# Spectral filter and MLP on one core: filter products that read the transform's sums in PSUM, and the product's high part cast by ScalarE instead of VectorE

## Chip, cores, metric

One NeuronCore of a Trainium2 chip. The metric is the device time of one launch in microseconds, a median over runs; lower is better. The kernel before takes 2332.32 us (median of 3 runs, 2330.84 to 2332.87).

## What is computed

```python
x: (8, 3008, 256), filt_r, filt_i: (1505, 256), w_in: (256, 2048), w_out: (2048, 256)
X = np.fft.rfft(x, axis=1)
Y = X * (filt_r + 1j * filt_i)[None]
a = np.fft.irfft(Y, n=3008, axis=1).reshape(24064, 256)
h = a @ w_in
g = h / (1 + exp(-1.702 * h))
out = g @ w_out
```

All in fp32. A sequence of 3008 is transformed along 64 x 47 points: a first stage over 64, a second over 47, the product with the filter, and the two inverse stages.

## The kernel before

**MLP.** The 24064 tokens are 48 tiles (8 batches b, 6 tiles t each), of 512 columns, or 384 for t = 5 in batches 0, 2, 4 and 6. A tile has 16 chunks of the hidden width, fc. For each chunk TensorE (PE) makes six products into a PSUM tile `h` (L844), ScalarE (ACT) applies the activation twice, once rounded into `gh` (L848) and once in place in PSUM (L849), VectorE (DVE) subtracts the two into the low part `gl` (L850), and PE makes six products from `gh` and `gl` into two sums `o` (L869). Every operand of precision is split like this: a high part that TensorE reads as it is (type fp32r), and a low part that holds the rest.

**Transform of the next batch.** While PE works through the tiles of batch b - 1, a generator `fft(b)` is stepped between the chunks (a table of costs, `COSTS`, says after which chunk the next step is issued), so the transform of batch b runs beside the MLP. Its first stage (`packed`, for b > 1, or `thrice`) leaves `a_d` in DRAM. Its second stage has 16 groups i for each of 7 batches (112 in all), and `forward(i)` and `backward(i - 1)` alternate:

- `forward(i)`: two products `s2` on PE (k = 0, 1; L588 to L591), each with 48 useful rows on one side of the PSUM tile and the correction on the other. `merge` (L599, L600) has ACT copy the correction into `c_buf` and DVE add the sum into `c_buf`, in SBUF. DVE then multiplies with the filter in `f_buf`: L608 and L613 into `u_buf` (the parts with filt_i), L614 for both k at once into `c_buf` (filt_r). GpSimd (POOL) adds the two (L615). DVE casts the high part into `zy` (L619, once for each k), and POOL subtracts it for the low part (L620).
- `load(i + 2)` (L577, POOL's queue) brings the next input from `a_d`, and `load_f(i + 2)` the filter (SP's queue, L210).
- `backward(i)`: two products `i2` on PE, merged in the same way into `b`, which is stored to `b_d` from ACT's queue (L636).

**From a transform to its first tile.** When the last group of batch b is stored, `signal(b, 0)` or `turned_signal(b, 0)` makes the first tile of that batch: `br` is loaded from `b_d` (SP), split by ACT (L785) and POOL (L786), multiplied on PE into `i1` (L307 to L309), turned by DVE into `zt` (L794), sent through DRAM (`z_d`, then four loads of `y`, all on SP), and split by ACT (L726) and POOL (L727) into `y`. The first chunk of tile (b, 0), `h_b_0_0`, needs it.

**PSUM.** The tiles `s1`, `s2`, `i1` and `i2` share a ring of three banks (`ps_f`); `h` has three banks (two, and a shared one) from tile 6 on; the two `o` have one each.

**Order.** Instructions are issued by the Python code, and a scheduler at build time then sets the order in which they stand in each engine's queue; `keep_in_program_order` pins some of them. On the chip each queue is in order: an instruction that waits holds what stands behind it.

The change touches `forward` only.

Of the kernel before, what the change touches and what calls it, by code (L numbers as in the profile page):

```python
# [14 lines left out]
ALU = mybir.AluOpType  # L15
# [6 lines left out]
Q = 112  # L22
# [147 lines left out]
def tile_kernel(  # L170
# [9 lines left out]
    nc = tc.nc  # L180
# [17 lines left out]
    def ring(kind, shape, name):  # L198

        own = {"f": (ps_f, 3), "h": (ps_h, 2)}[kind]  # L200
        turn_of[kind] += 1
        if shared[0] == kind and turn_of[kind] % (own[1] + 1) == 0:
            return ps_x.tile(shape, F32, tag="x", name=name)
        return own[0].tile(shape, F32, tag=kind, name=name)
# [99 lines left out]
    zy = []  # L304
# [157 lines left out]
    def fft(b):  # L462
# [111 lines left out]
        def load(i):  # L574
            for k in range(2):
                src = a_d[k, 4 * i : 4 * i + 4].rearrange("q n d -> n q d")
                nc.gpsimd.dma_start(zy[0][64 * k : 64 * k + 48, i % 2].rearrange("p k s d -> p (k s) d"), src)  # L577

        def load_f(i):
            for k in range(2):  # L580
                load_in(f_buf[64 * k : 64 * k + 48, 2 * (i % 2) : 2 * (i % 2) + 2], fs[i])

        def second(i, m, src, name, k):

            pin = tc.keep_in_program_order
            ps = ring("f", [P, 2, D], f"{name}_{b}_{i}_{k}")
            if i == 0:
                pin(nc.tensor.matmul(ps[:, 0], de_sb[:, k, m + 1], src[:, k, 0], start=True, stop=True))  # L588
                nc.tensor.matmul(ps[:, 1], de_sb[:, k, m], src[:, k, 1], start=True, stop=True)
            else:  # L590
                pin(nc.tensor.matmul(ps, de_sb[:, k, m], src[:, k], start=True, stop=True))  # L591
            return ps

        def sides(k):
            return slice(64 * k, 64 * k + 48), slice(64 - 64 * k, 112 - 64 * k)

        def merge(k, ps, dst):
            h, o = sides(k)
            nc.scalar.copy(dst[h], ps[o])  # L599
            nc.vector.tensor_tensor(dst[h], ps[h], dst[h], ALU.add)  # L600

        def forward(i):

            u1, u2 = c_buf[i % 3], u_buf[i % 2]
            fr = f_buf[:Q, 2 * (i % 2) : 2 * (i % 2) + 2]
            f_r, f_i = fr[:, :, 0, :], fr[:, :, 1, :]
            merge(0, second(i, 0, zy[0][:, i % 2], "s2", 0), u1)
            nc.vector.tensor_tensor(u2[64:Q], u1[0:48], f_i[0:48], ALU.mult)  # L608
            yield
            merge(1, second(i, 0, zy[0][:, i % 2], "s2", 1), u1)  # L610
            if i + 2 < 16:
                load(i + 2)
            nc.vector.scalar_tensor_tensor(u2[0:48], u1[64:Q], -1.0, f_i[64:Q], ALU.mult, ALU.mult)  # L613
            nc.vector.tensor_tensor(u1, u1[:Q], f_r, ALU.mult)  # L614
            nc.gpsimd.tensor_tensor(u1, u1, u2, ALU.add)  # L615
            y = zy[0][:, 2 + i % 2]
            for k in range(2):
                h, o = sides(k)
                nc.vector.tensor_copy(y[h, k], u1[h])  # L619
                nc.gpsimd.tensor_tensor(y[o, k], u1[h], y[h, k].bitcast(F32), ALU.subtract)  # L620
            if i + 2 < 16:
                load_f(i + 2)
            yield
# [24 lines left out]
        for i in range(17):  # L648
            if i < 16:
                yield from forward(i)  # L650
            if i:
                yield from backward(i - 1)
# [367 lines left out]
```

## Time and profile before

| what | value |
|---|---|
| median of 3 runs | 2332.32 us (2330.84 to 2332.87) |
| profiled execution: its time | 2332.26 us |
| profiled execution: span of the instructions | 2330.2 us |
| DVE busy | 1622.9 us (70%), 2426 instructions |
| ACT busy | 1458.4 us (63%), 2686 instructions |
| POOL busy | 1155.2 us (50%), 1019 instructions |
| DMA | 293.44 MB, mean 126 GB/s |

The span runs from the first to the last instruction; 2.06 us of the execution's time lie outside it. Busy shares are means over the whole span; the transform of a batch takes part of it, the second stage of batches 1 to 7 lying between 177 us and 2026 us. A row of the profile gives the line of the kernel, the engine, the operation, `out<-in` by tile names without numbers, and a shape as partitions x elements. PEld is the load of TensorE's weights. An engine name with a q (ACTq, SPq) marks what its queue issues, DMAs above all.

### The profile page before, as it was taken

To read this page: it belongs to the slowest core of one execution; us is meant where nothing else is said; L and a number is where in the kernel's file an instruction comes from. 1 tells how busy PE (TensorE), PEld (TensorE's weight loads), DVE (VectorE), ACT (ScalarE), POOL (GpSimd) and SP (SyncE) were. 2 spreads that over 40 slices of the span, in tenths; PEclk is the share of its full clock that TensorE was granted. 3 is DMA by queue.
4 is the path that set the end of the run, shared out by engine and by line. 5 is a ranking of instruction groups with operands and counts; after the bars stand their busy time and mean duration, and the time that the engine had idled before them with its cause. 6 is when DMAs were issued, how large, how long until landed. Compare 5 with 4: busy or idle time off the path is not lost.

```text
span 2330.2 us, 32285 instructions
## 1 busy us (share of the span) xinstructions
PE 2321.9 (100%) x10620; PEld 1942.6 (83%) x10620; DVE 1622.9 (70%) x2426; ACT 1458.4 (63%) x2686; POOL 1155.2 (50%) x1019
## 2 busy tenths in 40 slices
PE   9999999999999999999999999999999999999999
PEld 7888898888888889888888888988888888888887
DVE  7978876688666885678856887568876688633332
ACT  6666667666675666756676666766657566555553
POOL 3035546466564665556654555636647365422220
PEclk9999999999999999999999999999999999999999
DMA  9265545556455654555545554555655465421200
GB/s 340 82 193 110 111 107 143 133 136 134 108 148 128 144 136 131 152 121 138 133 133 141 130 128 121 148 136 128 138 133 143 115 141 121 111 62 55 82 28 19
DMA packets 191958, 293.44 MB, mean 126 GB/s; under 512 B 18736, under 2 KB 127920, under 8 KB 191792
## 3 DMA queue, kind: packets, MB, share of 16 engines
q1 hardware_dynamic: 115088, 180.89, 27.1%
q0 software_dynamic: 46592, 44.05, 11.6%
q10 hardware_dynamic: 30112, 66.44, 11.1%
q8 instruction: 85, 1.39, 0.3%
q14 instruction: 81, 0.66, 0.1%
HBM read 176.49 MB, written 114.82 MB: 125 GB/s over the span
## 4 chain that ended last, share of the span: by engine, by line
PE 95%; DVE 2%; DMA 2%; ACT 1%; issue 1%; ACTq 0%; POOL 0%; SPq 0%; DVEq 0%; POOLq 0%
PE h L844 43%; PE o L869 43%; PE i L591 2%; PE s L591 2%; PE s L540 1%; PE i L309 1%; PE i L307 1%; PE i L308 1%; PE i L709 1%; DMA x<-in_x_dram 0%; DVE gl L850 0%; PE s L388 0%; DVE w_tu L277 0%; DMA fs<-f_y 0%; DMA w<-in_w_out_dram 0%
## 5 line engine op out<-in xcount | busy, mean ns | idle before, releaser
L844 PE MATMUL h<-y,wi 128*128 128x512 f32 (+1 forms) x4608 | 1178.2, 385 | 0.6 <-DVE gl L850 0.5
L844 PEld LDWEIGHTS h<-y,wi 128*128 128x128 f32 x4608 | 858.9, 188 | 166.0 <-DVE gl L850 1.9
L850 DVE TENSOR_TENSOR gl<-h,gh 128x512 fp32r<-128x512 f32 (+1 forms) x768 | 521.3, 679 | 487.4 <-ACT h L849 452.9
L869 PE MATMUL o<-gh,wo 128*128 128x512 f32 (+1 forms) x3072 | 838.7, 385 | 0.8 <-ACT gh L848 0.8
L848 ACT ACTIVATE gh<-h 128x512 fp32r<-128x512 f32 (+1 forms) x768 | 452.7, 589 | 583.7 <-PE h L844 448.5
L869 PEld LDWEIGHTS o<-gh,wo 128*128 128x128 f32 x3072 | 573.4, 188 | 111.2 <-ACT gh L848 1.5
L869 PE MATMUL o<-gl,wo 128*128 128x512 f32 (+1 forms) x1536 | 481.7, 385 | 0.5 <-DVE gl L850 0.5
L849 ACT ACTIVATE h<-h 128x512 f32<-128x512 f32 (+1 forms) x768 | 448.4, 584 | 0.0
L620 POOL TENSOR_TENSOR zy<-c_buf,zy 48x512 fp32r<-48x512 f32 x224 | 316.3, 1412 | 75.0 <-DVE zy L619 62.7
L869 PEld LDWEIGHTS o<-gl,wo 128*128 128x128 f32 x1536 | 287.5, 188 | 56.4 <-DVE gl L850 1.2
L615 POOL TENSOR_TENSOR c_buf<-c_buf,u_buf 112x512 f32<-112x512 f32 x112 | 144.8, 1293 | 229.8 <-DVE c_buf L614 229.8
L577 POOL DMA_DIRECT2D zy<-a_d x224 | 130.7, 588 | 232.0 <-PE s L591 92.5
L786 POOL TENSOR_TENSOR bl<-br,bh 128x512 fp32r<-128x512 f32 x70 | 94.5, 1363 | 201.5 <-ACT bh L785 168.5
L600 DVE TENSOR_TENSOR c_buf<-s,c_buf 48x512 f32<-48x512 f32 x224 | 154.1, 688 | 34.0 <-ACT c_buf L599 29.4
L599 ACT COPY c_buf<-s 48x512 f32<-48x512 f32 x224 | 130.4, 582 | 70.8 <-PE s L591 57.6
L599 ACT COPY b<-i 48x512 f32<-48x512 f32 x224 | 130.4, 582 | 58.2 <-PE i L591 46.4
L600 DVE TENSOR_TENSOR b<-i,b 48x512 f32<-48x512 f32 x224 | 153.8, 687 | 15.1 <-ACT b L599 10.2
L543 DVE TENSOR_TENSOR a<-s,a 64x512 f32<-64x512 f32 x144 | 99.0, 688 | 61.9 <-ACT a L542 58.7
L619 DVE CAST zy<-c_buf 48x512 fp32r<-48x512 f32 x224 | 109.7, 490 | 39.1 <-POOL c_buf L615 34.1
L727 POOL TENSOR_TENSOR y<-y 128x512 fp32r<-128x512 f32 (+1 forms) x76 | 92.6, 1225 | 59.5 <-ACT y L726 48.1
L608 DVE TENSOR_TENSOR u_buf<-c_buf,f_buf 48x512 f32<-48x512 f32 x112 | 109.2, 975 | 3.8
L542 ACT CAST a<-s 64x512 fp32r<-64x512 f32 x144 | 83.8, 582 | 40.7 <-PE s L540 28.6
(138 smaller groups left out, 1867.4 us busy)
## 6 DMA issues: line engine op xcount, KB each, us to landing
f_buf<-fs SPq DMA_DIRECT2D x224, 192.0 KB, 3.5
zy<-a_d POOLq DMA_DIRECT2D x224, 192.0 KB, 3.7
a_d<-a ACTq DMA_DIRECT2D x144, 256.0 KB, 3.0
x<-in_x_dram SPq DMA_DIRECT2D x47, 512.0 KB, 5.5
br<-b_d SPq DMA_DIRECT2D x94, 256.0 KB, 4.5
out_dram<-out SPq DMA_DIRECT2D x43, 512.0 KB, 3.5
b_d<-b ACTq DMA_DIRECT2D x112, 192.0 KB, 2.8
z_d<-zt SPq DMA_DIRECT2D x40, 512.0 KB, 2.7
```

What stands on the lines that cost most here:

```text
L577: nc.gpsimd.dma_start(zy[0][64 * k : 64 * k + 48, i % 2].rearrange("p k s d -> p (k s) d"), src)
L599: nc.scalar.copy(dst[h], ps[o])
L600: nc.vector.tensor_tensor(dst[h], ps[h], dst[h], ALU.add)
L608: nc.vector.tensor_tensor(u2[64:Q], u1[0:48], f_i[0:48], ALU.mult)
L615: nc.gpsimd.tensor_tensor(u1, u1, u2, ALU.add)
L619: nc.vector.tensor_copy(y[h, k], u1[h])
L620: nc.gpsimd.tensor_tensor(y[o, k], u1[h], y[h, k].bitcast(F32), ALU.subtract)
L844: ins = nc.tensor.matmul(ps[:, :w], wi_sb[half][:, wk, kc, c], y[:, yk, kc, :w], start=n == 0, stop=n == 5)
L848: nc.scalar.activation(gh[:, :w], ps[:, :w], AF.Gelu_apprx_sigmoid)
L849: gelu.append(nc.scalar.activation(ps[:, :w], ps[:, :w], AF.Gelu_apprx_sigmoid).ins)
L850: nc.vector.tensor_tensor(gl[:, :w], ps[:, :w], gh[:, :w].bitcast(F32), ALU.subtract)
L869: ins = nc.tensor.matmul(pos[m][:, :w], wb[:, P * m : P * m + P], g[:, :w], start=first_one, stop=last_one)
```

## The change

In `forward(i)` the sum is no longer moved to SBUF: DVE adds the correction in place, in the PSUM tile `ps` of the product. The three multiplications become four, of 48 rows each, which read the sum in PSUM and the filter in SBUF, and follow each k's sum at once. The two casts into `zy` go from DVE to ACT. The load of the next input is issued behind the multiplications of k = 1 rather than ahead of them.

```diff
             f_r, f_i = fr[:, :, 0, :], fr[:, :, 1, :]
-            merge(0, second(i, 0, zy[0][:, i % 2], "s2", 0), u1)
-            nc.vector.tensor_tensor(u2[64:Q], u1[0:48], f_i[0:48], ALU.mult)
-            yield
-            merge(1, second(i, 0, zy[0][:, i % 2], "s2", 1), u1)
+            for k in range(2):
+                h, o = sides(k)
+                ps = second(i, 0, zy[0][:, i % 2], "s2", k)
+                nc.scalar.copy(u1[h], ps[o])
+                nc.vector.tensor_tensor(ps[h], ps[h], u1[h], ALU.add)
+                if k:
+                    nc.vector.scalar_tensor_tensor(u2[o], ps[h], -1.0, f_i[h], ALU.mult, ALU.mult)
+                else:
+                    nc.vector.tensor_tensor(u2[o], ps[h], f_i[h], ALU.mult)
+                nc.vector.tensor_tensor(u1[h], ps[h], f_r[h], ALU.mult)
+                if k == 0:
+                    yield
             if i + 2 < 16:
                 load(i + 2)
-            nc.vector.scalar_tensor_tensor(u2[0:48], u1[64:Q], -1.0, f_i[64:Q], ALU.mult, ALU.mult)
-            nc.vector.tensor_tensor(u1, u1[:Q], f_r, ALU.mult)
             nc.gpsimd.tensor_tensor(u1, u1, u2, ALU.add)
             y = zy[0][:, 2 + i % 2]
             for k in range(2):
                 h, o = sides(k)
-                nc.vector.tensor_copy(y[h, k], u1[h])
+                nc.scalar.copy(y[h, k], u1[h])
                 nc.gpsimd.tensor_tensor(y[o, k], u1[h], y[h, k].bitcast(F32), ALU.subtract)
```

Since a scheduler sets the order, the queues change in more places than the diff shows. Lines behind the change move by six (L844 becomes L850, L848 becomes L854, L869 becomes L875).

ACT's queue in batch 4, from chunk 8 of tile (3, 2) on (`gh_3_2_8` is the high part of chunk 8; `s2_4_4_0` the product of group 4, k = 0). Before:

```order
L848 ACTIVATE gh_3_2_8_10004<-h_3_2_8_9997 128x512
L849 ACTIVATE h_3_2_8_9997<-h_3_2_8_9997 128x512
L599 COPY c_buf1_83<-s2_4_4_1_9960 48x512
L848 ACTIVATE gh_3_2_9_10028<-h_3_2_9_10021 128x512
L849 ACTIVATE h_3_2_9_10021<-h_3_2_9_10021 128x512
L599 COPY b_4_1_9906<-i2_4_3_0_9993 48x512
L599 COPY b_4_1_9906<-i2_4_3_1_10015 48x512
L636 DMA b_d4_9505<-b_4_1_9906 48x1024
L848 ACTIVATE gh_3_2_10_10066<-h_3_2_10_10059 128x512
```

And now:

```order
L610 COPY c_buf1_83<-s2_4_4_0_10007 48x512
L610 COPY c_buf1_83<-s2_4_4_1_10013 48x512
L854 ACTIVATE gh_3_2_9_10081<-h_3_2_9_10074 128x512
L855 ACTIVATE h_3_2_9_10074<-h_3_2_9_10074 128x512
L599 COPY b_4_1_9958<-i2_4_3_0_10046 48x512
L854 ACTIVATE gh_3_2_10_10120<-h_3_2_10_10113 128x512
L855 ACTIVATE h_3_2_10_10113<-h_3_2_10_10113 128x512
L642 DMA b_d4_9553<-b_4_1_9958 48x1024
L625 CAST zy_1451<-c_buf1_83 48x512 x2
L599 COPY b_4_1_9958<-i2_4_3_1_10068 48x512
L854 ACTIVATE gh_3_2_11_10138<-h_3_2_11_10131 128x512
```

The two casts of group 4 now stand between the activations of chunks 10 and 11, with a copy behind them.

PE's queue where tile (2, 5) ends and tile (3, 0), the first that needs the transform of batch 3, begins (`o_2_5` are the sums of the old tile, `s1_4` products of the first stage of batch 4). Before:

```order
L540 MATMUL s1_4_2_1_8829<-e1_4_2_8752,t1_two_3258 128x512
L844 MATMUL h_3_0_0_8842<-y_3_0_8479,wi_0_583 128x512
L869 MATMUL o_2_5_0_8495<-gl_2_5_13_8769,wo_1_984 128x384
L869 MATMUL o_2_5_1_8496<-gl_2_5_13_8769,wo_1_984 128x384
L869 MATMUL o_2_5_0_8495<-gh_2_5_14_8788,wo_1_984 128x384
```

And now:

```order
L540 MATMUL s1_4_2_0_8848<-e0_4_2_8773,t1_two_3274 128x512
L875 MATMUL o_2_5_0_8543<-gl_2_5_15_8867,wo_1_984 128x384
L875 MATMUL o_2_5_1_8544<-gl_2_5_15_8867,wo_1_984 128x384
L540 MATMUL s1_4_2_1_8877<-e1_4_2_8800,t1_two_3274 128x512
L850 MATMUL h_3_0_0_8890<-y_3_0_8527,wi_0_583 128x512
L850 MATMUL h_3_0_1_8916<-y_3_0_8527,wi_0_583 128x512
L850 MATMUL h_3_0_2_8955<-y_3_0_8527,wi_0_583 128x512
L540 MATMUL s1_4_3_0_8940<-e0_4_3_8853,t1_two_3274 128x512
```

The first product of tile (3, 0) stood ahead of the last 14 products into the old tile's sums; now it stands behind all of them. From the last inverse product of batch 3, `i2_3_15_1`, to that first product the queue holds 166 matmuls of 384 columns and 19 of 512 before, and 122 and 13 now.

SP's queue in the same stretch. Before:

```order
L210 DMA br_3_0_8480<-b_d3_6817 64x4x256 x2
L210 DMA z_d_3_0_8620<-zt_3_0_8567 128x1024
L210 DMA y_3_0_8479<-z_d_3_0_8620 32x8x128
L210 DMA x_4_2_8677<-in_x_dram 128x1024
L210 DMA y_3_0_8479<-z_d_3_0_8620 32x8x128 x3
```

And now:

```order
L210 DMA br_3_0_8528<-b_d3_6849 64x4x256 x2
L210 DMA z_d_3_0_8668<-zt_3_0_8615 128x1024
L210 DMA x_4_2_8725<-in_x_dram 128x1024
L210 DMA y_3_0_8527<-z_d_3_0_8668 32x8x128 x4
L210 DMA br_3_1_8806<-b_d3_6849 64x4x256 x2
```

The load of `x_4_2` moves from behind the first of the four loads of `y` to ahead of all four.

## Rows read from the trace of the kernel before

**Rows 1.** The page, part 1: TensorE's busy time, share and instructions.

```profile
PE 2321.9 (100%) x10620; PEld 1942.6 (83%) x10620; DVE 1622.9 (70%) x2426; ACT 1458.4 (63%) x2686; POOL 1155.2 (50%) x1019
```

**Rows 2.** Busy time by stretch: us, PE, PEld, DVE, ACT, POOL, granted clock, DMA.

```profile
177.00:333.00 156.00, 155.30 (x741) 131.79 (x741) 131.77 (x207) 97.42 (x180) 84.23 (x79) 1.00 0.50 111
722.00:888.00 166.00, 166.00 (x740) 137.91 (x739) 142.76 (x206) 105.05 (x193) 101.39 (x94) 1.00 0.56 130
177.00:2026.00 1849.00, 1848.30 (x8360) 1549.55 (x8360) 1377.85 (x2039) 1193.72 (x2180) 1052.45 (x932) 1.00 0.54 130
```

**Rows 3.** Timeline, 1041 to 1049 us: start, duration, engine, line, operation, [idle before].

```profile
1041.06 1.52 PE L844 MATMUL h<-y,wi 128*128 128x512 f32 x6
1041.93 0.68 DVE L600 TENSOR_TENSOR c_buf<-s,c_buf 48x512 f32<-48x512 f32 x1 [0.31 <-ACT c_buf L599]
1042.42 0.62 PE L869 MATMUL o<-gl,wo 128*128 128x512 f32 x2
1042.62 0.60 ACT L848 ACTIVATE gh<-h 128x512 fp32r<-128x512 f32 x1 [0.72 <-DVE c_buf L600]
...
1047.41 0.39 PE L591 MATMUL i<-zy,de_sb 128*128 128x512 f32 x1
...
1048.99 0.84 PE L869 MATMUL o<-gh,wo 128*128 128x512 f32 x3
```

**Rows 4.** Groups by line and shape: count, busy us, mean ns, idle before and its releaser.

```profile
L600 DVE TENSOR_TENSOR c_buf<-s,c_buf 48x512 f32<-48x512 f32 x224 | 154.1, 688 | 34.0 <-ACT c_buf L599 29.4
L619 DVE CAST zy<-c_buf 48x512 fp32r<-48x512 f32 x224 | 109.7, 490 | 39.1 <-POOL c_buf L615 34.1
L608 DVE TENSOR_TENSOR u_buf<-c_buf,f_buf 48x512 f32<-48x512 f32 x112 | 109.2, 975 | 3.8
L613 DVE SCALAR_TENSOR_TENSOR u_buf<-c_buf,f_buf 48x512 f32<-48x512 f32 x112 | 88.8, 793 | 3.4
L614 DVE TENSOR_TENSOR c_buf<-c_buf,f_buf 112x512 f32<-112x512 f32 x112 | 85.2, 760 | 1.9
L528 ACT CAST e<-x 64x512 fp32r<-64x512 f32 x72 | 44.6, 620 | 11.8 <-POOL e L529 8.9 <-POOL x L522 1.4
L457 DVE SCALAR_TENSOR_TENSOR u_buf<-s,f_y 48x512 f32<-48x512 f32 x8 | 5.5, 693 | 0.2
```

**Rows 5.** Timeline, 186.7 to 189.5 us, of POOL, DVE and PE.

```profile
186.79 3.02 POOL L620 TENSOR_TENSOR zy<-c_buf,zy 48x512 fp32r<-48x512 f32 x2
187.01 1.66 DVE L613 SCALAR_TENSOR_TENSOR u_buf<-c_buf,f_buf 48x512 f32<-48x512 f32 x1
188.71 0.69 DVE L850 TENSOR_TENSOR gl<-h,gh 128x512 fp32r<-128x512 f32 x1
189.45 1.66 PE L844 MATMUL h<-y,wi 128*128 128x512 f32 x6 [0.46 <-DVE gl L850]
```

**Rows 6.** Timeline, 887.9 to 921.2 us, the chain from batch 3's transform to tile (3, 0).

```profile
887.91 0.40 PE L591 MATMUL i<-zy,de_sb 128*128 128x512 f32 x1
...
890.17 0.31 ACTq L636 DMA_DIRECT2D b_d<-b  x1
897.38 1.14 ACT L785 CAST bh<-br 128x512 fp32r<-128x512 f32 x2 [1.40 <-DMA br<-b_d]
904.62 0.70 DVE L794 STREAM_TRANSPOSE zt<-i 128x512 f32<-128x512 f32 x1
905.35 0.34 SPq L210 DMA_DIRECT2D z_d<-zt  x1
909.35 1.90 SPq L210 DMA_DIRECT2D y<-z_d  x3
918.05 0.62 ACT L726 CAST y<-y 128x512 fp32r<-128x512 f32 x1
919.66 2.55 POOL L727 TENSOR_TENSOR y<-y 128x512 fp32r<-128x512 f32 x2
921.20 0.40 PE L844 MATMUL h<-y,wi 128*128 128x512 f32 x1
```

**Rows 7.** DMA issues, 903 to 922 us: KB each, median us from issue to landing.

```profile
y<-z_d SPq DMA_DIRECT2D x4, 128.0 KB, 5.0
```

**Rows 8.** The same of 1757 to 1774 us, where batch 6 hands over.

```profile
y<-z_d SPq DMA_DIRECT2D x4, 128.0 KB, 2.9
```

## The prediction

> **What bounds the kernel.** I read the page's engine shares first: TensorE is busy for 2321.9 us of the 2330.2 us span, the others 70% or less [rows 1]. A busy share of PE can mislead, so the timeline comes next. Six products of 512 columns start at 1041.06 and the seventh at 1042.42, 0.2267 us apiece with no gap [rows 3]. Then the stretches: from 177 us (where the second stage of the first transform that the change touches begins) to 2026 us, PE is without work for 1849.00 - 1848.30 = 0.70 us, at a granted clock of 1.00, which is the 2.4 GHz level [rows 2]. The changed lines issue the same products with the same columns. So the time is this row of products plus the gaps in it, and the change can give back 0.7 us at most; all that can move the time upwards is a product that comes to wait. By DVE's 142.76 us of 166.00 in a second stage against ACT's 105.05 [rows 2], DVE is the fuller of the two, yet neither sets the time.
>
> **The change, part by part.** I work against the profiled execution, 2332.26 us, which is 0.06 us under the median.
>
> *DVE, per group.* Before: two sums of 688 ns, 975 and 793 and 760 for the three multiplications, two casts of 490 [rows 4]: 4884 ns. After: two sums and four multiplications of 48 rows. The trace has the same multiplication from PSUM in the first transform, 693 ns [rows 4]. A sum that is written to PSUM has no row on DVE; I bound it by the 688 ns of the same sum into SBUF and by the 975 of the dearest operation here, and take 688, since shape and inputs are the same. 2 x 688 + 4 x 693 = 4148 ns, so DVE saves 0.74 us a group, 82 us over 112 groups. PE's products cover all of it: worth nothing by itself. At 975 the saving is 18 us, and the cover is the same.
>
> *ACT, per group.* Two casts of 620 ns, the row of a cast from SBUF to SBUF [rows 4], come on: 139 us over the kernel. In a second stage of 16 groups ACT goes from 105.05 to 105.05 + 16 x 1.24 = 125 of 166 us, and DVE from 142.76 to 131. Again no engine is full. The casts bring a wait: on DVE they waited 34.1 us in all for POOL's addition [rows 4]. Now ACT waits, with the copy of an inverse product and the activations behind it. What hides it: `gh` of a chunk ended at 1042.62 + 0.60 = 1043.22 and was first used two chunks later, at 1048.99, 5.8 us of margin [rows 3]. Two casts (1.24) and the mean wait per group (34.1 / 112 = 0.3) fit. Taken as nothing.
>
> *The sums' stay in PSUM.* `s2` of k = 0 was free when its sum ended, 1041.93 + 0.68 = 1042.61; the ring of three comes back to that bank with the fourth product, at 1047.41, 4.8 us later [rows 3]. Two multiplications more are 1.4 us; 3.4 are left. Taken as nothing, up to 1 us in some groups if a `gl` comes in between. The Trainium skill, "PSUM — Partial Sum Buffer", section "Summary: rules for kernel authors", speaks against the change: "Evacuate promptly — 2 MiB is tight". By that rule PE would be held by the ring and the sum would grow; the 4.8 us above are the row against it.
>
> *POOL and SP.* They issue what they issued. `load` stands behind two more multiplications in the code, but its wait is for the product on PE, as before.
>
> *A collision that goes.* L613, 793 ns on average [rows 4], took 1.66 us at 187.01 while POOL's subtraction ran; `gl` was late and PE waited 0.46 us at 189.45 [rows 5]. The new multiplications read one operand from PSUM, as the sums of L600 do, which keep to 688 ns beside the same POOL [rows 4]. I take -0.5 us.
>
> *The hand-over from a transform to its first tile.* This is where the change costs. The transform ends later in PE's queue, so less work stands between its last product and the first product that needs its result. For batch 3 the queue held 166 products of 384 and 19 of 512 columns there, which took 921.20 - 887.91 = 33.29 us [rows 6]; with 0.2267 for the wide ones, a narrow one is (33.29 - 4.31) / 166 = 0.1746 us. Now there are 122 and 13: 21.30 + 2.95 = 24.2 us of cover. The chain that has to fit, step by step [rows 6 to 8]: the product to `br` split, 887.91 to 897.38, 9.5 us (up to 0.9 more, as ACT's store of `b_d` now stands behind a chunk's activations); on to the end of `zt`, 904.62 + 0.70, 7.9; from `z_d`'s issue at 905.35 to the last issue of `y`, 909.35 + 2/3 x 1.90 = 910.6, 5.3, or 4.6 now that no load of `x` stands between the four; its landing, 5.0 beside other loads, 2.9 without; the first split of `y`, 0.62. From 25.6 to 29.3 us. I take 27.2 (half of the ACT delay, 4.6, a landing of 4.0, since the load of `x_4_2` now runs just ahead): 3.0 us more than the cover. Behind the first product, the second of chunk 0 comes after three others, 0.9 us, but needs POOL's half, 2.55 / 2 = 1.3: 0.4 more. **+3.4 us.** In the order before, products of the old tile filled that hole; now the old tile has none left.
>
> *The other hand-overs.* Counted alike, batches 4 and 6 have 138 products of 512 (31.3 us), batch 5 has 156 and 13 (30.2), batch 7 has 156 and 7 (28.8), against 25.6 to 29.3: mostly covered, +0.3 in all. Batches 1 and 2 don't go through `z_d`; nothing.
>
> **Sum:** 2332.26 - 0.5 + 3.4 + 0.3 = 2335.5, and with the bounds of the hand-over (1.3 to 5.1 short) 2333.4 to 2337.6. All the guesses of that chain lean towards waiting, so I forecast 2335.0. A difference under 0.2% (4.7 us) can't be told from no change, so this is "within".
>
> **The rivals.**
>
> 1. *The hand-over of batch 3 holds longer: slower.* SP's queue is in order, and the load of `x_4_2` now stands ahead of all four loads of `y`. If its buffer is not free when `z_d` has landed, or if it takes the transfers' time from them, each microsecond goes straight into PE's hole. It decides once batch 3 loses 5.2 us or more (4.7 + 0.5): the long end of the chain (5.1 + 0.4) already does, 2337.5, and 3 us of SP waiting gives 2340.5. For it: the landing of 5.0 us beside such a load [rows 7] against 2.9 [rows 8]. Against it: the load has the time of `z_d`'s own landing to get out of the way. Chance 0.22.
> 2. *The hand-over fits after all.* If `y` lands in 2.9 us and POOL gets to its part at once, the shortfall is near 1 us and the freed collision pays for half: 2331.7 to 2332.4. `y` was split at 918.05, in ACT's order, perhaps well after it lands [rows 6]. Chance 0.10.
> 3. *ACT holds the activations.* A cast that waits for POOL's addition delays two chunks' `gh`. It needs more than 5.8 us of delay in a row [rows 3]; if one group in ten lost 1 us, 2343. Chance 0.05.
> 4. *The ring holds PE.* With the 3.4 us of margin used up in one group of ten and 1 us lost in each, again 2343. Chance 0.03. (It is where the page quoted above would lead.)
> 5. *Faster by over 0.2%.* Rows 2 leave 0.7 us to gain; only an error of reading allows it. Chance 0.03.
>
> The forecast has the remaining 0.57; with rival 2, within 0.2%: 0.67. Slower: 0.22 + 0.05 + 0.03 = 0.30. Faster: 0.03. The range runs from 2331.3 (rival 2 and the spread of runs) to 2340 (most of rival 1); the forecast's own is 2332.5 to 2337.
>
> **What the profile after would show.** DVE near 1541 us busy, ACT near 1597; the multiplications at 684 to 700 ns without the long ones; L620 on POOL shorter than before, with fewer collisions. PE without a gap but near 925 us, where it waits some 3 us for ACT's or POOL's split of `y`, and nothing of the like at the other batches. Wrong would be: PE waiting for an activation in the middle of a second stage (rivals 3, 4), SP's load of `x` waiting ahead of `y` (rival 1), or no wait at 925 us at all (rival 2).

## The result, and the profile after

The changed kernel takes 2352.44 us (median of 4 runs, 2350.91 to 2353.04), the one before beside it 2332.6 (2330.84 to 2333.09): a ratio of 1.0085, with an interval of 1.0068 to 1.0103. It is **slower, by 20 us**. The forecast was 2335.0 and no difference that can be measured, with a range up to 2340.0; both were wrong.

The page of the kernel after, part 1, as in [rows 1]:

```profile
PE 2331.3 (99%) x10620; PEld 1942.7 (83%) x10620; DVE 1542.3 (66%) x2314; ACT 1593.2 (68%) x2910; POOL 1116.2 (47%) x1019
```

The loads of the engines came out as worked out (DVE 1541, ACT 1597), and the durations within 2%. These are the groups that answer to [rows 4]; the sum written to PSUM has a row now, 700 ns:

```profile
L611 DVE TENSOR_TENSOR s<-s,c_buf 48x512 f32<-48x512 f32 x224 | 156.9, 700 | 30.4 <-ACT c_buf L610 24.5
L616 DVE TENSOR_TENSOR c_buf<-s,f_buf 48x512 f32<-48x512 f32 x224 | 154.2, 688 | 3.0
L613 DVE SCALAR_TENSOR_TENSOR u_buf<-s,f_buf 48x512 f32<-48x512 f32 x112 | 77.6, 693 | 3.6
L625 ACT CAST zy<-c_buf 48x512 fp32r<-48x512 f32 x224 | 138.5, 619 | 85.6 <-POOL c_buf L621 81.9
```

VectorE has 81 us less to do, and the kernel is 20 us longer. Where they went is read by stretches, as in [rows 2] (us, PE, PEld, DVE, ACT, POOL, granted clock, DMA share, GB/s):

```profile
177.00:333.00 156.00, 153.69 (x729) 129.37 (x728) 125.74 (x189) 114.02 (x207) 77.22 (x76) 1.00 0.50 111
722.00:888.00 166.00, 166.00 (x739) 137.76 (x738) 120.98 (x179) 119.25 (x215) 88.92 (x89) 1.00 0.60 119
890.00:905.00 15.00, 14.01 (x74) 12.56 (x74) 10.95 (x18) 11.36 (x24) 5.95 (x5) 1.00 0.51 161
924.00:941.00 17.00, 12.42 (x41) 8.79 (x40) 11.24 (x17) 9.44 (x19) 12.84 (x11) 0.80 0.79 242
941.00:1180.00 239.00, 239.00 (x1060) 198.01 (x1059) 167.56 (x247) 170.88 (x305) 130.83 (x123) 1.00 0.57 125
1180.00:1240.00 60.00, 58.55 (x254) 46.94 (x253) 35.21 (x53) 42.36 (x77) 35.42 (x28) 1.00 0.52 148
1750.00:1812.00 62.00, 59.52 (x257) 47.39 (x256) 35.85 (x53) 42.66 (x78) 35.72 (x28) 1.00 0.51 144
```

Most of the second stage runs full (722 to 888, 941 to 1180). PE lacks work in the second stage of batch 1, at the end of the later ones, and above all where batches 3, 4 and 6 hand over to their first tile (924 to 941, 1180 to 1240, 1750 to 1812).

**A ledger for all that follows.** Between the starts of two successive products of PE lie 0.2267 us for 512 columns [rows 3], or 0.1733 for 384, when PE is full. All time beyond that, summed over the products, I call lost (the few products of other widths, nearly all of them in the start, count with their usual step; only the level of the start hangs on that). It is 18.6 us before and 38.9 after; the difference, 20.3, is that of the spans (2350.5 - 2330.2), so the ledger holds everything. It is taken from the one profiled execution of each kernel, while the column of medians is over all its runs. It is split by place: the start (to 177 us), batch 1's transform (177 to 400), the hand-overs (from the last inverse product of batch 2, 3, ... to 15 us behind the first product of its first tile), and the rest. Lost us:

| kernel | median us | start | batch 1 | hand-overs | rest |
|---|---|---|---|---|---|
| before | 2332.6 | 15.4 | 1.6 | 1.0 | 0.6 |
| after | 2352.4 | 15.7 | 3.6 | 15.5 | 4.1 |
| e1 casts on VectorE | 2353.0 | 15.6 | 5.1 | 17.3 | 2.6 |
| e2 casts alone | 2334.3 | 15.7 | 3.3 | 1.1 | 0.7 |
| e3 paced | 2339.9 | 15.4 | 4.0 | 3.1 | 3.5 |
| e4 four banks | 2347.3 | 15.5 | 3.7 | 1.0 | 13.2 |
| e5 before, four banks | 2338.2 | 15.3 | 1.6 | 1.2 | 6.4 |
| e6 sums in SBUF | 2351.0 | 16.4 | 7.3 | 2.4 | 13.5 |
| e7 split product | 2351.4 | 15.5 | 7.1 | 2.7 | 12.7 |
| e8 paced, casts on VectorE | 2335.9 | 15.5 | 4.7 | 1.9 | 1.5 |
| e9 before, paced | 2334.3 | 15.3 | 1.6 | 1.3 | 2.9 |
| e10 low half on VectorE | 2350.0 | 15.8 | 4.0 | 11.3 | 5.8 |
| e11 banks held | 2382.2 | 15.8 | 4.2 | 34.1 | 17.0 |
| e12 split by columns | 2337.4 | 15.3 | 4.2 | 2.4 | 0.6 |

Of the 20.3 us the hand-overs took 14.5 (batch 3 8.9, batch 4 2.4, batch 6 3.4, the others nothing), the rest of the second stages 3.5, batch 1 2.0, the start 0.3.

**Batch 3's hand-over**, 903 to 941 us, in the timeline, which answers to [rows 6]:

```profile
903.61 0.39 PE L591 MATMUL i<-zy,de_sb 128*128 128x512 f32 x1
912.79 1.14 ACT L791 CAST bh<-br 128x512 fp32r<-128x512 f32 x2 [2.61 <-DMA br<-b_d]
920.01 0.70 DVE L800 STREAM_TRANSPOSE zt<-i 128x512 f32<-128x512 f32 x1
920.75 0.34 SPq L210 DMA_DIRECT2D z_d<-zt  x1
921.13 0.43 SPq L210 DMA_DIRECT2D x<-in_x_dram  x1
923.71 2.76 SPq L210 DMA_DIRECT2D y<-z_d  x4
...
926.67 0.98 PE L875 MATMUL o<-gh,wo 128*128 128x384 f32 x4 [0.39 <-ACT gh L854]
...
928.52 0.47 PE L540 MATMUL s<-e,t_two 128*128 128x512 f32 x1 [0.24 <-DVE a L544]
929.68 1.27 POOL L529 TENSOR_TENSOR e<-x,e 64x512 fp32r<-64x512 f32 x1
930.03 1.14 ACT L732 CAST y<-y 128x512 fp32r<-128x512 f32 x2 [0.24 <-DMA y<-z_d]
930.64 0.47 PE L540 MATMUL s<-e,t_two 128*128 128x512 f32 x1 [1.00 <-DVE a L544]
930.95 0.86 PE L850 MATMUL h<-y,wi 128*128 128x512 f32 x3
931.02 1.28 POOL L522 TENSOR_TENSOR ev<-x 128x512 f32<-128x512 f32 x1
932.38 1.27 POOL L529 TENSOR_TENSOR e<-x,e 64x512 fp32r<-64x512 f32 x1
932.67 0.47 PE L540 MATMUL s<-e,t_two 128*128 128x512 f32 x1 [0.86 <-DVE a L544]
933.72 2.50 POOL L733 TENSOR_TENSOR y<-y 128x512 fp32r<-128x512 f32 x2
935.04 6.28 PE L850 MATMUL h<-y,wi 128*128 128x512 f32 x15 [1.90 <-DMA out_dram<-out]
941.16 1.07 PE L875 MATMUL o<-gh,wo 128*128 128x512 f32 x4
```

From the last inverse product to the first of tile (3, 0) the chain took 930.95 - 903.61 = 27.34 us; 33.29 us of queue stood there before [rows 6], now 24.1 us of products and 3.3 us lost. None of PE's waits in these 3.3 us is put down to `y`: they are for an activation of the old tile (0.39) and for VectorE's part in the next batch's first stage (0.24, 1.00). `y` would not have been there earlier, though: its first split starts at 930.03 and takes about 0.6 us, so the two waits end together, at about 930.6, and no run parts them. That hole had been seen, and a second had not. The low half of `y` is POOL's, and when the first split was done, POOL was in the first of three first-stage instructions of the next batch, and the two others stood ahead of `y`'s: 933.72 instead of soon after 930.6. PE's next products start at 935.04, and the wait that the profile puts down to a store is really for this half: the first of its two instructions ends about 933.72 + 2.50 / 2 = 934.97.

### The profile page after: what moved, and what is told of

Read it like the earlier page. It is cut to its first block, busy times and chain, and to the rows that moved or that the text cites. A ratio compares the mean times of both kernels' runs of the same rounds, so it can differ in the third digit from the quotient of the medians.

```text
span 2350.5 us, 32421 instructions
## 1 busy us (share of the span) xinstructions
PE 2331.3 (99%) x10620; PEld 1942.7 (83%) x10620; DVE 1542.3 (66%) x2314; ACT 1593.2 (68%) x2910; POOL 1116.2 (47%) x1019
## 3 DMA queue, kind: packets, MB, share of 16 engines
q1 hardware_dynamic: 115088, 180.89, 27.2%
q8 instruction: 85, 1.39, 0.3%
## 5 line engine op out<-in xcount | busy, mean ns | idle before, releaser
L850 PE MATMUL h<-y,wi 128*128 128x512 f32 (+1 forms) x4608 | 1184.0, 386 | 4.7 <-DVE gl L856 2.3
L850 PEld LDWEIGHTS h<-y,wi 128*128 128x128 f32 x4608 | 860.4, 188 | 174.7 <-DVE gl L856 6.3
L875 PE MATMUL o<-gh,wo 128*128 128x512 f32 (+1 forms) x3072 | 839.6, 385 | 4.0 <-ACT gh L854 4.0
L854 ACT ACTIVATE gh<-h 128x512 fp32r<-128x512 f32 (+1 forms) x768 | 452.6, 589 | 436.8 <-PE h L850 364.0
L875 PEld LDWEIGHTS o<-gh,wo 128*128 128x128 f32 x3072 | 573.0, 188 | 116.2 <-ACT gh L854 7.0
L875 PE MATMUL o<-gl,wo 128*128 128x512 f32 (+1 forms) x1536 | 483.1, 385 | 0.9 <-DVE gl L856 0.9
L875 PEld LDWEIGHTS o<-gl,wo 128*128 128x128 f32 x1536 | 287.2, 188 | 57.3 <-DVE gl L856 2.5
L626 POOL TENSOR_TENSOR zy<-c_buf,zy 48x512 fp32r<-48x512 f32 x224 | 288.3, 1287 | 91.1 <-ACT zy L625 78.5
L600 DVE TENSOR_TENSOR b<-i,b 48x512 f32<-48x512 f32 x224 | 153.4, 685 | 67.3 <-ACT b L599 63.0
L625 ACT CAST zy<-c_buf 48x512 fp32r<-48x512 f32 x224 | 138.5, 619 | 85.6 <-POOL c_buf L621 81.9
L792 POOL TENSOR_TENSOR bl<-br,bh 128x512 fp32r<-128x512 f32 x70 | 89.7, 1292 | 183.7 <-ACT bh L791 168.1
L611 DVE TENSOR_TENSOR s<-s,c_buf 48x512 f32<-48x512 f32 x224 | 156.9, 700 | 30.4 <-ACT c_buf L610 24.5
L616 DVE TENSOR_TENSOR c_buf<-s,f_buf 48x512 f32<-48x512 f32 x224 | 154.2, 688 | 3.0
L610 ACT COPY c_buf<-s 48x512 f32<-48x512 f32 x224 | 130.3, 582 | 34.0 <-PE s L591 24.2
```

Of the source, the lines that this page charges most:

```text
L610: nc.scalar.copy(u1[h], ps[o])
L611: nc.vector.tensor_tensor(ps[h], ps[h], u1[h], ALU.add)
L616: nc.vector.tensor_tensor(u1[h], ps[h], f_r[h], ALU.mult)
L625: nc.scalar.copy(y[h, k], u1[h])
L850: ins = nc.tensor.matmul(ps[:, :w], wi_sb[half][:, wk, kc, c], y[:, yk, kc, :w], start=n == 0, stop=n == 5)
L854: nc.scalar.activation(gh[:, :w], ps[:, :w], AF.Gelu_apprx_sigmoid)
```

## The experiments

Two theories stood at the start. **H**: the sums stay longer in the ring of three PSUM banks, so the second stage's products stand later in PE's queue and the hand-overs lose their cover. **A**: the casts on ScalarE hold the activations.

**e1.** The changed kernel with the casts back on VectorE.

```diff
-                nc.scalar.copy(y[h, k], u1[h])
+                nc.vector.tensor_copy(y[h, k], u1[h])
```

> The changed kernel with the two casts given back to VectorE (L625 as before); the sums stay in PSUM. Theory H (hand-over: the sums' longer stay in the ring of three PSUM banks makes the second stage end later in TensorE's queue, and the first tile of the next batch finds too little old work to cover its chain): as slow as the changed kernel, 2342 to 2354 us, with the gap near 925 us again, since in this kernel's queue batch 3 has only 23.4 us of products for a chain that took 27.3. Theory A (ScalarE's casts hold the activations and with them TensorE): back to 2331 to 2335 us.

Measured: 2353.02 us, ratio 1.0086 (1.0070 to 1.0101). The hand-overs lose 17.3 us, much as in the changed kernel. So the casts are not the cause of the 20 us: theory A falls as the main one.

**e2.** The reverse: the kernel before with the casts alone on ScalarE (the same line, edited the other way).

> The kernel before with only the two casts moved to ScalarE; sums and products as before, in SBUF. Theory H: 2331 to 2334 us, no gap at a hand-over (its queue keeps 33.7 us of products for batch 3). Theory A: 2340 to 2352 us, with TensorE waiting for activations.

Measured: 2334.34 us, ratio 1.0009 (1.0000 to 1.0018). That is 0.3 us above what H allowed. The casts cost about 2 us, most of it in batch 1 (3.3 lost against 1.6), in one wait of 1.60 us for a `gl` at 219.16.

**e3.** The changed kernel, with the transform's steps issued earlier between the chunks. `upto` is the point up to which a batch's steps are spread.

```diff
-        ... - ((18 if b > 1 else 12) * width(6 * b + 5) if b else 26)
+        ... - ((20 if b > 1 else 18) * width(6 * b + 5) if b else 26)
```

> The whole change, and only the pacing of the transforms moved: batch 2's transform is issued to end 6 chunks earlier, batches 3 to 7 two chunks earlier. Its queue then has 34 us or more of products at every hand-over from batch 3 on. Theory H: 2331 to 2335 us (what is lost within batch 1's second stage, some 2 us, stays). Theory A: at least 2343 us, since ScalarE has the same casts in the same stages.

Measured: 2339.94 us, ratio 1.0034 (1.0021 to 1.0046), between the two theories and outside both of their ranges. The hand-overs lose 3.1 us instead of 15.5: the chain is the same, the cover is back (34.87 us from the last inverse product to tile (3, 0)'s first product in this trace, against 27.34). The stretch 924 to 941 us has no hole any more and the full clock (PE's busy time follows the comma):

```profile
924.00:941.00 17.00, 17.00 (x80) 14.57 (x80) 11.52 (x18) 13.49 (x27) 9.97 (x8) 1.00 0.47 120
```

**e4 and e5.** The ring keeps its fourth bank to the end, in the changed kernel and, as a control, in the one before. It has that bank from tile 2 to tile 6 in every kernel here, so in batch 1's second stage the ring has four banks and `h` two; the three banks hold from tile 6 on. The edit also issues the first products of a chunk one chunk ahead instead of two.

```diff
-        if n == 6 * NFC:
-            shared[0] = "h"
-        while begun <= min(n + 1 + (n >= 6 * NFC), len(turns) - 1):
+        while begun <= min(n + 1 + 0, len(turns) - 1):
```

> The whole change, with the fourth PSUM bank left in the ring of the transform's tiles to the end (it goes to the ring of h at tile 6 otherwise), and the first products of a chunk one chunk ahead instead of two. The bank taken from h may cost something by itself; run e5_before_ring4 is the kernel before with the same edit. Theory H: e4 and e5 differ by under 4 us, since with four banks the sums' stay no longer sets where the second stage ends (batch 3's last inverse product stands within 2 us of the same place in both queues). Theory A: e4 is 10 us or more slower than e5.

> The kernel before with four banks in the transform's ring and two for h throughout, and one chunk of lead: the control of e4. 2331 to 2345 us by either theory; only the difference to e4 counts.

Measured: 2347.32 us, ratio 1.0064 (1.0049 to 1.0079), and 2338.18, ratio 1.0025 (1.0015 to 1.0035). The hand-overs are as before the change (1.0 us lost), and the second stage of batch 3 lasts as long as before: from its first `s2` product to its last 153.6 us (152.0 in e5), 153.4 before, 165.5 after. So the ring's three banks are what makes the stage longer. But the two kernels still differ by 9.1 us, where H alone allowed 4: a miss for H, and close to the 10 of A. PE's waits for `gh` don't bear A out, 0.8 us in e4 and 0.7 in e5. What is left is seen in TensorE's waits (line waited for: us, times, longest), first of e4, then of e5:

```profile
PE h L850 <- DVE gl L856: 8.6, 13, 1.4
```

```profile
PE h L844 <- DVE gl L850: 4.1, 6, 1.3
```

With two banks for `h`, PE waits for a low half `gl`, and in the changed kernel `gl` is late twice as often; this is 4.5 of the 9.1 us. The timeline of the kernel after shows why, in batch 1's stage, where `h` has two banks too (all of DVE's instructions of the stretch, one activation and the product that waits):

```profile
214.26 0.71 DVE L611 TENSOR_TENSOR s<-s,c_buf 48x512 f32<-48x512 f32 x1
...
214.63 0.59 ACT L855 ACTIVATE h<-h 128x512 f32<-128x512 f32 x1
...
215.00 0.68 DVE L615 TENSOR_TENSOR u_buf<-s,f_buf 48x512 f32<-48x512 f32 x1
...
215.70 0.68 DVE L616 TENSOR_TENSOR c_buf<-s,f_buf 48x512 f32<-48x512 f32 x1
...
216.41 0.69 DVE L613 SCALAR_TENSOR_TENSOR u_buf<-s,f_buf 48x512 f32<-48x512 f32 x1
...
217.12 0.69 DVE L616 TENSOR_TENSOR c_buf<-s,f_buf 48x512 f32<-48x512 f32 x1
...
217.85 0.69 DVE L856 TENSOR_TENSOR gl<-h,gh 128x512 fp32r<-128x512 f32 x1
...
218.59 0.73 PE L850 MATMUL h<-y,wi 128*128 128x512 f32 x2 [1.39 <-DVE gl L856]
```

The activation was done at 214.63 + 0.59 = 215.22; its `gl` stands behind four multiplications and starts at 217.85; PE waits 1.39 us for the bank that this `gl` sets free. This suggests a second cost, theory **K**: no engine is full, but VectorE's instructions come in a block ahead of a `gl`. The place alone doesn't show that the four multiplications are to blame: e2, with the old ones, waits 1.60 us there. Its `gl` stands behind two sums and two multiplications, one of which takes 1.65 us, and the sums start a microsecond later, since ScalarE's copies for them stand behind the two casts.

**e6.** The changed kernel with the sum in SBUF again: no multiplication reads a bank any more, the four multiplications of 48 rows stay.

```diff
-                nc.vector.tensor_tensor(ps[h], ps[h], u1[h], ALU.add)
+                nc.vector.tensor_tensor(u1[h], ps[h], u1[h], ALU.add)
...
-                nc.vector.tensor_tensor(u1[h], ps[h], f_r[h], ALU.mult)
+                nc.vector.tensor_tensor(u1[h], u1[h], f_r[h], ALU.mult)
```

> The changed kernel (four multiplications of 48 rows, casts on ScalarE), but the sum goes to SBUF, where the multiplications read it: the stay in PSUM alone is undone. Theory H: most of the loss goes, 2332 to 2340 us (its queue has 30.0 us of products for batch 3, 38.3 for batches 4 and 6, 32.2 and 30.8 for 5 and 7, against a chain of 27.3); the multiplications become longer again where POOL runs beside them. Theory A: 2345 us or more.

Measured: 2351.03 us, ratio 1.0079 (1.0062 to 1.0096). A miss for H as it then stood, and in A's range. Yet PE waits 7.0 us for `gl` in it and 1.8 for `gh`, and the loss has moved: the hand-overs lose 2.4 us instead of 15.5, batch 1 and the rest of the stages 20.8 instead of 7.7.

**e7.** To find which part of that edit costs it: e2 with nothing but L614 split in two, at its old place.

```diff
-            nc.vector.tensor_tensor(u1, u1[:Q], f_r, ALU.mult)
+            for k in range(2):
+                h, o = sides(k)
+                nc.vector.tensor_tensor(u1[h], u1[h], f_r[h], ALU.mult)
```

> The kernel before with the casts on ScalarE (2334.3 us so measured), and one more edit: the product with the filter's real part, one instruction of 112 rows, is two of 48 rows at the same place. The sums go to SBUF and leave PSUM as early as before. Theory H (the sums' stay in PSUM is the cost): nothing happens, 2333 to 2337 us. Theory K (what delays VectorE is the number and order of its instructions between a sum and the low half of the activation behind it, whatever memory the products read): it falls like the kernel with the products from SBUF (2351.0 us), 2345 to 2353 us, with TensorE waiting for the low half of an activation in the second stage of batches 2 and 3.

Measured: 2351.41 us, ratio 1.0082 (1.0068 to 1.0095). One instruction made into two costs 17 us over e2, with no product that reads a bank: what K expected, and a miss for H. PE's waits for `gl` are its largest item, 7.4 us (1.6 in e2). Its groups on DVE, and one place in its timeline:

```profile
L616 DVE TENSOR_TENSOR c_buf<-c_buf,f_buf 48x512 f32<-48x512 f32 x224 | 172.8, 771 | 5.1
```

```profile
851.57 2.99 POOL L788 TENSOR_TENSOR bl<-br,bh 128x512 fp32r<-128x512 f32 x2 [0.42 <-issue]
851.81 1.60 DVE L616 TENSOR_TENSOR c_buf<-c_buf,f_buf 48x512 f32<-48x512 f32 x1
...
854.17 0.94 DVE L613 SCALAR_TENSOR_TENSOR u_buf<-c_buf,f_buf 48x512 f32<-48x512 f32 x1
...
855.14 0.69 DVE L852 TENSOR_TENSOR gl<-h,gh 128x512 fp32r<-128x512 f32 x1
...
855.88 1.43 PE L846 MATMUL h<-y,wi 128*128 128x512 f32 x5 [1.19 <-DVE gl L852]
```

A multiplication with both inputs in SBUF takes 1.60 us beside POOL's subtraction, and another 0.94; the `gl` behind them starts at 855.14 and PE waits 1.19 us. The Trainium skill, "SBUF — State Buffer", section "Who interferes with whom", says that an instruction of VectorE with two SBUF inputs contends with one of GpSimd that reads SBUF, and one with at most one such input, outside the engine's two-port modes, does not; the traces agree (the products of L616 and L608 take 771 and 905 ns on average here, and those of the changed kernel from PSUM, L616 and L615, 688 and 684; of its 224 in L616 none took over 0.70 us).

**e8 and e9.** The paced version with the casts on VectorE, and the pacing alone in the kernel before.

> The paced version (2339.9 us) with the casts of the filtered product back on VectorE. If ScalarE's casts are what the paced version still pays (1.6 us and more at 216 and 318 us, and activations later elsewhere): 2336 to 2338 us. If what is left is VectorE's own queue (theory K), 110 us more of work on it makes it worse: 2341 to 2346 us.

> Control for the paced version: the kernel before with the earlier pacing alone. Its hand-overs were covered, so theory H gives 2331 to 2334 us, no change beyond 0.1%. If the denser second stage has a price of its own: 2335 to 2338 us, and most of what the paced version still loses is the pacing's.

Measured: e8 2335.9 us, ratio 1.0014 (1.0005 to 1.0023); e9 2334.34, ratio 1.0009 (1.0000 to 1.0017). So the casts are what the paced version still paid (0.1 us below the range given for that); K, as e8's expectation put it, missed: more work on VectorE made nothing worse there. e9 lies 0.3 us above H's range. The earlier pacing costs 2 us by itself (1.0 us lost at each of two waits near 505 and 555 us). Each against the kernel before that ran beside it, e3 is 7.9 us above, e8 3.5 and e9 1.9: of the 7.9, about 4.4 are the casts', 1.9 the pacing's and 1.6 the sums' and their products'. What the casts cost depends on the rest: 2 us in the kernel before (e2), 4 in the paced one, nothing in the changed one (e1), where the holes lie elsewhere.

**e10.** The changed kernel with the low half of `y` made by VectorE, to price POOL's part at the hand-over.

```diff
-        nc.gpsimd.tensor_tensor(to[:, 1, m], src, to[:, 0, m].bitcast(F32), ALU.subtract)
+        nc.vector.tensor_tensor(to[:, 1, m], src, to[:, 0, m].bitcast(F32), ALU.subtract)
```

> The changed kernel with the low half of y at the hand-over made by VectorE in place of POOL, whose queue held it until 933.7 us. The first hole of batch 3's hand-over (3 us) stays, the second (some 2.4 us) goes. If the products behind it still run at 0.43 us apiece: 2349 to 2350.5 us. If they are back at 0.23 us, so that the lower clock came from the second hole: 2346.5 to 2348 us. If POOL's half cost only the 0.4 us of the prediction: 2352 us.

Measured: 2349.99 us, ratio 1.0075 (1.0063 to 1.0088). The timeline of PE and a window of this kernel:

```profile
931.89 0.98 PE L850 MATMUL h<-y,wi 128*128 128x512 f32 x3
933.57 5.29 PE L850 MATMUL h<-y,wi 128*128 128x512 f32 x15 [0.70 <-DVE y L733]
```

```profile
934.00:937.50 3.50, 3.50 (x10) 2.71 (x9) 3.38 (x5) 0.00 (x0) 2.27 (x2) 0.51 0.86 324
```

The wait for the low half falls to 0.70 us; batch 3's hand-over loses 6.5 us instead of 9.2. The products behind it still run at the lower clock, for a shorter time: 15 of them from 933.57 until the next product at 938.71, 5.14 us where 15 x 0.2267 = 3.40 would do, so 1.7 lost. So POOL's queue was worth about 2.7 us there, not the 0.4 of the prediction, and about 1 us of this is the shorter time at the lower clock. That clock doesn't hang on the second hole alone.

**e11.** H by itself: e2 with two tiny instructions per group that read the sums' banks behind the multiplications, and do nothing else (48 rows by 2 elements).

```diff
+            nc.vector.tensor_tensor(last_sb[64:Q], ps[64:Q, :, :1], u2[64:Q, :, :1], ALU.mult)
...
             nc.vector.tensor_tensor(u1, u1[:Q], f_r, ALU.mult)
+            nc.vector.tensor_tensor(last_sb[0:48], ps[0:48, :, :1], u1[0:48, :, :1], ALU.mult)
```

> The kernel before with the casts on ScalarE (2334.3 us), its products unchanged and fed from SBUF; added are two instructions of VectorE per group, of 48 rows by 2 elements, that read the PSUM banks of the sums behind the products. They hold the banks as long as the changed kernel does, and do nothing else. Theory H (the stay alone makes the second stage end late and opens the hand-overs): like the changed kernel or worse, 2347 to 2365 us, with batch 3's next tile waiting for its y. Theory K (VectorE's order of products alone): 2334 to 2339 us, without holes at the hand-overs.

Measured: 2382.2 us, ratio 1.0213 (1.0196 to 1.0230): 48 us over e2, and 17 more than the upper end that H gave. The hand-overs lose 34.1 us, batch 3's alone 19.0. The stretch of batch 3's hand-over in it:

```profile
924.00:962.00 38.00, 26.74 (x100) 20.36 (x99) 15.04 (x24) 18.06 (x35) 23.98 (x19) 0.73 0.51 148
```

How long the banks are held, from the start of an `s2` product to the end of the last instruction that reads its bank, mean over the 96 groups of batches 2 to 7 (k = 0, k = 1), beside batch 3's second stage: its length, first `s2` product to last, what the ledger holds as lost in it, and the time of the products (without what is lost) that are left behind its last inverse product up to tile (3, 0), the cover:

| kernel | stay, k = 0 | stay, k = 1 | second stage of batch 3 | lost in it | cover left |
|---|---|---|---|---|---|
| before | 2.5 us | 2.4 us | 153.4 us | 0.1 us | 33.1 us |
| e2 casts alone | 2.8 | 2.5 | 152.3 | 0.2 | 33.7 |
| e7 split product | 4.0 | 3.9 | 161.3 | 5.8 | 30.0 |
| after | 4.6 | 5.3 | 165.5 | 0.2 | 24.1 |
| e11 banks held | 4.9 | 6.1 | 175.6 | 4.7 | 15.4 |

From the two kernels with the short stay, which hardly differ, to e11: the longer the banks are held, the longer the stage, also without what is lost in it, and the less cover is left. (In e7 most of the added length is PE waiting, so its 17 us are not the hold's in the main.) e11 holds the banks somewhat longer than the changed kernel, and loses more: with 15.4 us of cover PE stands 7.9 us in all for POOL's part in the next batch's first stage. It shows H without the products from PSUM. The two tiny instructions take 0.31 us of VectorE a group (163 and 145 ns); e12, next, adds 0.23 us a group to the same kernel without holding a bank.

**e12.** The counterpart of e7: the same product in two instructions, each of 112 rows and half of the columns.

```diff
-            nc.vector.tensor_tensor(u1, u1[:Q], f_r, ALU.mult)
+            for k in range(2):
+                nc.vector.tensor_tensor(u1[:, k], u1[:Q, k], f_r[:, k], ALU.mult)
```

> Counterpart of the split product (2351.4 us): the same product is again two instructions, but each has all 112 rows and half of the columns, so that VectorE's time for it hardly grows. If the time of the two 48-row instructions beside POOL (0.77 us each where one of 112 rows took 0.81) was what made the low half of the activation late: 2334 to 2339 us. If the number of instructions was: 2345 us or more.

Measured: 2337.35 us, ratio 1.0021 (1.0012 to 1.0031). Its two instructions take 522 ns each:

```profile
L615 DVE TENSOR_TENSOR c_buf<-c_buf,f_buf 112x256 f32<-112x256 f32 x224 | 108.0, 522 | 1.2
```

That is 1.04 us a group where e7 needs 1.54 and e2 0.81. So the number of instructions is not what costs; VectorE's time between a sum and the next `gl` is what is left of K. The split by rows also lengthened the hold of the banks (4.0 and 3.9 us in e7, 2.9 and 2.5 here), and no run parts the two. And with 3 us lost for 0.23 us a group here, and 17 for 0.73 in e7, the greater part of e11's 48 is left to the hold.

## Why the prediction was wrong

**What bounds the kernel.** Right: the time is PE's row of products and the holes in it, and the ledger accounts for the whole difference by holes and slow products. Also right: 81 us less on VectorE are worth nothing, since PE covered them, and the collision of [rows 5] went (no wait of PE near 189 us after the change, 0.46 us before). That this is due to the products from PSUM isn't shown alone: it goes too in e2, where only the casts moved. And another wait came in the same stage, 1.39 us at 218.59, so the -0.5 was not gained. The lower bound of the sum left out the 0.4 us of POOL's half that the upper one has; that changes nothing here.

**The sums' stay in PSUM, "taken as nothing": wrong.** The step set 1.4 us for two more multiplications against a margin of 4.8. The stay grew from 2.5 and 2.4 us to 4.6 and 5.3, so by 2.1 and 2.9: the multiplications of one sum queue behind the other sum and its multiplications (as from 214.26 on; a `gl`, the delay that the step allowed for, stands between a sum and its last multiplication in only 16 of the 192). Even 2.9 is within the 4.8. So the margin was the wrong measure: it was read between places that an order laid out around the short hold had given. That PE is not seen waiting for a bank (722 to 888 us: 166.00 us busy of 166.00) did not make it free. With the longer hold the order laid out at build time has the products later, and PE fills the place with products of the old tile: the second stage of batch 3 is 12 us longer, full of work, and that work is then missing at the hand-over. The rule of the Trainium skill quoted in the prediction ("Evacuate promptly", "PSUM — Partial Sum Buffer") pointed to the right place. What the runs add is the way it took here, the order and not a wait: e4 and e11 show it, e3 mends it. How the scheduler weighs a held bank, no run shows. Rival 4 named the ring, at 0.03, but with waits in the middle of a stage as its picture.

**The hand-over of batch 3, +3.4: the mechanism right, the size too small.** The chain took 27.34 us, where 27.2 was worked out, and the cover was 24.1, where 24.2 was counted. So the 3.0 us stood, with some luck: PE's wait just ahead of the first product was for the first stage of the next batch, which the sum didn't have, and it ended when `y` was there. But the step ended at the first product. The ledger has 9.2 us there, 8.9 more than before: 3.3 up to the first product, 3.2 from there to 935.04, and 2.7 behind it:

- POOL's half of `y` was taken at 0.4 us, from its duration. It stood in POOL's queue behind instructions for the next batch, and the 3.2 us end with it. e10 prices it at 2.7, with its share of the next item.
- The clock had no term at all. The 15 products from 935.04 are followed by the next at 941.16: 6.12 us instead of 15 x 0.2267 = 3.40, so 2.7 lost, at a granted clock of about half (last section).

**The other hand-overs, +0.3: wrong, they took 5.8** (batch 4 2.4, batch 6 3.4). Their cover to the first product was rightly counted, 31.28 us in the trace of batch 4, and that product came without a wait. Most of that batch's loss came ten us later, when the old tile's products had run out and the new tile had no activation yet:

```profile
1232.15 0.39 PE L850 MATMUL h<-y,wi 128*128 128x512 f32 x1
1233.32 0.73 PE L875 MATMUL o<-gh,wo 128*128 128x512 f32 x2 [0.79 <-ACT gh L854]
```

The cover has to last until the new tile's first activations are out, not only to its first product.

**ScalarE's casts, "taken as nothing": nearly.** 0 to 4 us, by the kernel around them (e1, e2, e3 against e8). The wait for POOL's addition was 81.9 us in all, 0.7 a group, where 0.3 was taken. **VectorE's order, not in the prediction at all:** `gl` behind a block of other instructions, as at 217.85. It may have a part in the 5.5 us of batch 1 and the rest; how these divide between it, the casts and the late end of the stages was not tried apart. The prediction compared the engines' totals, 131 of 166 us, and not the longest run of instructions ahead of a `gl`.

The rivals gave 0.30 to "slower", most of it to the loads of `y` on SP behind a load of `x`. SP didn't wait for that load: `z_d` was issued at 920.75 and landed in 2.9 us, and the four loads follow at 923.71. They landed in 3.8 us (median), and 4.0 was in the sum:

```profile
y<-z_d SPq DMA_DIRECT2D x4, 128.0 KB, 3.8
```

What went wrong is one omission, that a queue which is laid out in advance turns a longer hold into a later place, a hand-over that was followed to the first product only, and a term read from a duration where the place in a queue decided. The profile's sign "nothing of the like at the other batches" failed with them.

None of the versions beats the kernel before. After 177 us it loses 3.2 us in all, so there is hardly anything to gain here.

## What to carry to other kernels

Price a buffer's longer hold by the queue that is laid out around it: compare where the last product of the stage stands before and after, and what stock of other work is left behind it, up to the moment when the new work feeds itself. A saving on an engine that isn't the bound can still lengthen the longest run of its instructions ahead of the one that the bound waits for; look at that run, not at the sum. When such a change is wanted all the same, shift the stage earlier with it: that took back 12.5 of the 20 us here.

## What the hardware showed that was not expected

TensorE's clock fell after the hole at the hand-over. Three stretches of the changed kernel:

```profile
926.60:931.00 4.40, 2.90 (x10) 1.67 (x11) 4.12 (x7) 3.77 (x8) 4.12 (x4) 1.00 0.88 233
931.00:935.00 4.00, 1.28 (x5) 0.51 (x3) 3.81 (x7) 1.71 (x4) 3.82 (x4) 0.85 0.98 357
935.00:941.00 6.00, 5.96 (x15) 4.71 (x16) 1.77 (x3) 1.44 (x3) 2.46 (x2) 0.53 0.65 188
941.00:945.00 4.00, 4.00 (x19) 3.31 (x18) 2.16 (x4) 3.95 (x9) 1.94 (x2) 1.00 0.00 0
```

PE was busy for 2.90 of 4.40 us and then for 1.28 of 4.00; the granted clock was still 1.00 in the first and 0.85 in the second, and 0.53, near the 1.2 GHz level, in the 6 us in which PE was full again. At 941 us it was back at 1.00. So a hole can be paid a second time, after it ends: here with 2.7 us, and in e11 with about 3 us behind the last hole of batch 3's hand-over (15 products from 953.88 on, each some 0.2 us late). The shorter holes of batches 4 and 6, 0.79 us the one shown above, left the stretches around them at 1.00. The length of one hole doesn't decide: e6 and e7 both wait 1.2 us near 856 us, with the same 21.6 us busy of 24 (838 to 862 us), at a mean granted clock of 0.93 in e6 and 1.00 in e7.

A sum written back to PSUM in place cost VectorE 700 ns, hardly more than the 688 into SBUF, and the multiplications from PSUM 684 to 693 on average. The engine gained by it as meant; it was the bank that cost.
